# Attention scores as two 128-row products a head, last keys' weights stacked over 128 rows, and four pairs of heads instead of eight with values in whole float32

## The chip, the cores and the metric

The kernel runs on one core of one Trainium2 chip. The metric is the device time of one execution in microseconds. Its engines are TensorE (PE: matrix products; its weight loads are listed apart as PEld), VectorE (DVE), ScalarE (ACT), GpSimd (POOL) and the sync engine (SP), which issues nearly all DMAs here.

## The reference

Causal attention with a decay, then two feed-forward layers:

```python
scores = q @ k.T / 8 + cum[i] - cum[j]   # cum = cumsum(log(clip(f, 1e-4, 1))), keys j > i masked
attn = softmax(scores);  x = attn @ v    # 4 batches, 8 heads, 576 tokens, head dimension 64
x = (sigmoid(x @ w_gate) * (x @ w_val)) @ w_out      # 2304 tokens, 512 -> 1536 -> 512
h = x @ w_in;  out = (h * clip(h + 3, 0, 6) / 6) @ w_out2   # 512 -> 2048 -> 512
```

The weights arrive as float64 bits; everything else is float32.

## The kernel before, in words

**Numbers.** A float32 value is carried as two float32r parts, hi and lo, whose sum is exact, and a product is hi·hi + hi·lo + lo·hi: three TensorE products. `mm3` (L496) does this in the layers.

**Attention.** The work is 16 pairs of heads (`Pair`, pair 0 to 15), four to a batch. A pair has five steps: query tiles 0 to 3 of 128 queries with 128, 256, 384 and 512 keys, and the last 64 queries of both heads side by side ("the last queries") with all 576 keys. The steps run as a pipeline over `units` (L777 to L820): while step t makes scores (`scores`, L319) and exponentials (`expo`, L355: VectorE adds the decay and takes the row minimum, ScalarE exponentiates), step t-1 is normed (`norm`, L386, a GpSimd product), step t-2 is transposed on TensorE (`flip`, L393, with copies out of PSUM by ScalarE), and step t-3's weights meet the values (`values`, L439). Two thirds into a pair, `prep` (L233) transposes the next pair's q and k and splits them.

**Three settings by pair number (L742).** Pairs 0 to 7 (`WH`) take weights times values in float32 as it is, which the trace lists as two TensorE instructions a product; later pairs split the weights (VectorE, L436) and the values (GpSimd, `split_v`) into hi and lo. Pairs 0 to 6 (`UP`) run the steps from the first to the last, and a mask product on TensorE (L341) hides later keys; later pairs run them backwards, and GpSimd overwrites the decay instead (`hide`, L302). Pairs 0 to 6 (below `TW`) make a head's scores from three products over 64 rows (L337), the two heads in the upper and lower 64 rows. Pairs 7 to 15 stack q's hi and lo rows to 128 rows, stack k's hi twice (`stack_k`, on VectorE and GpSimd), and take one product over 128 rows (L326) and one over 64 rows with k's lo (L331). The last queries' scores are three products over 128 rows for each half of the keys, with q's hi and lo in block-diagonal tiles `qbd` (L348).

**What fills TensorE.** A weight's conversion takes three VectorE, two ScalarE or GpSimd steps and one more subtraction (`convert`, L95; while attention runs, GpSimd makes hi and lo, L61 and L62); 18 of them are spread over the steps from step 5 on. When they are done and a batch's attention is stored, groups of the gated layer's first part (`Filler`; tiles `pg`, `pv`, `po`; products of 256 columns) are put between attention's products; what is left of them follows after attention. Then come the rest of the gated layer (`ff1b`) and the second layer (`ff2`).

**Order.** The scheduler of the framework sets each engine's order when the program is built, from a simulated timeline; on the chip every engine runs its list in that order.

Of the kernel before, what the change touches and what calls it, by code (L numbers as in the profile page):

```python
# [12 lines left out]
ALU = mybir.AluOpType  # L13
# [7 lines left out]
def attn_moe_kernel(  # L21
# [33 lines left out]
    # float32 values are carried as two float32r parts, hi + lo, whose sum is exact;  # L55
    # a product is hi*hi + hi*lo + lo*hi.
# [21 lines left out]
    # rows 0..63 repeated in rows 64..127, for the two heads' last queries  # L78
# [14 lines left out]
    # A weight comes as float64 bits: float32 has the same sign, the exponent less 896 (a  # L93
    # product with 2^-112 of the high word read as float32), and the leading 23 mantissa bits.
# [18 lines left out]
    class Converter:  # L113
        """Weight halves still to be loaded and converted; run() emits some of them."""
# [4 lines left out]
        def cols(self, pool, tag, w, c0, nm):  # L119
            """256 columns of w, for products over its rows."""  # L120
# [6 lines left out]
        def rows(self, pool, tag, w, r0, nm):  # L127
            """256 rows of w."""
# [28 lines left out]
    ep = att.enter_context(tc.tile_pool(name="ep", bufs=7))  # L157
# [4 lines left out]
    qbd = [[const.tile([P, P], F32R, name=f"qbd{i}{j}") for j in range(2)] for i in range(2)]  # L162
    for i in range(2):
        for j in range(2):
            nc.vector.memset(qbd[i][j].bitcast(F32), 0.0)

    def cumulate():
        """Cumulative log decay, to DRAM."""
# [10 lines left out]
    def load_nat(src, b, hp, c0, c1, nm):  # L179
        """Rows c0 * 128 to c1 * 128, or to the end."""  # L180
        t = nat.tile([P, NKT, 2, D], F32, tag="nat", name=nm)
        n = min(c1, NQ)
        for j in range(2):
            nc.sync.dma_start(
                t[:, c0:n, j, :],
                src[b, 2 * hp + j, c0 * P : n * P, :].rearrange("(c p) d -> p c d", p=P),
            )
        if c1 > NQ:
            nc.sync.dma_start(
                t[:TAIL, NQ, :, :],  # L190
                src[b, 2 * hp : 2 * hp + 2, NQ * P : S, :].rearrange("h p d -> p h d"),
            )
        return t

    class Pair:
        """Two heads of one batch; its steps are the query tiles 0..3 and the last 64 queries, or
        some of them."""

        def __init__(self, i, b, hp, order, whole, two):
            self.i, self.b, self.hp, self.order, self.whole, self.two = i, b, hp, order, whole, two  # L200
            self.s0, self.s1 = min(order), max(order) + 1
            self.tail = self.s1 > NQ
            self.c0, self.c1 = self.s0 * P, S if self.tail else self.s1 * P
            # values' parts, after the steps that they wait for
            self.parts = {}
            for part, ss in ((0, (0, 1)), (1, (2, 3, NQ))):
                if ss[0] in order:
                    self.parts[max(ss, key=order.index)] = part
            self.x = None
            self.up = order[0] < order[-1]  # L210
            self.pemask = self.up or i < PM

        def load(self):
            self.qn = load_nat(q, self.b, self.hp, self.s0, self.s1, "qn")
            self.kn = load_nat(k, self.b, self.hp, 0, self.s1, "kn")
            self.vn = load_nat(v, self.b, self.hp, 0, self.s1, "vn")

        def load_decay(self):
            h0 = self.b * H + 2 * self.hp
            self.dc = a2.tile([P, 2, NQ * P], F32, tag="dc", name="dc")  # L220
            n = min(self.c1, NQ * P)
            for j in range(2):
                nc.sync.dma_start(self.dc[:, j, :n], cum_d[h0 + j : h0 + j + 1, :n].to_broadcast([P, n]))
# [9 lines left out]
        def prep(self):  # L233
            # q and k with head dimension on partitions, both heads; scores are negated
            q0, n = self.c0, min(self.c1, NQ * P)
            tq = psB.tile([P, 512], F32, tag="B", name="tq")
# [658 lines left out]
```

## Time and profile before

| | us |
|---|---|
| device time, median of 3 runs | 1126.88 (1120.99 to 1127.61) |
| the profiled execution: span from first to last instruction | 1124.5 |
| TensorE busy in the span | 1110.0 (99%) |
| VectorE, ScalarE, GpSimd busy | 592.4, 399.3, 339.7 |
| largest lines of the chain that ended last | TensorE 88%, VectorE 4%, DMA 3% |

The profiled execution's own time is its span of 1124.5 us, and no more of it is shown; it lies 2.4 us under the median and inside the range of the runs. Busy time on TensorE counts an instruction from its start to a modelled end, so neighbours overlap; what a product costs is read from one start to the next. Attention runs to about 395 us, the filling groups to about 500 us, the two layers to the end.

### The profile page before, as it was taken

What the parts mean: (1) busy time and instruction counts of PE and PEld (TensorE: products, weight loads), DVE (VectorE), ACT (ScalarE), POOL (GpSimd) and SP (SyncE); (2) the same over time, 40 slices, a digit from 0 to 9 for tenths busy, and PEclk for the clock granted to TensorE, in tenths of its full rate; (3) what the DMA queues carried; (4) which work ended last, traced back from release to release, by engine and by line L of the source; (5) the groups of instructions that cost most, each with busy time, mean ns of one, the idle gap of its engine ahead of it and who ended that gap; (6) DMA issues with size and microseconds to landing.
All of it is one profiled execution on the core that took longest, in us unless ns stands there. A gap on an engine that the chain in (4) does not pass through costs nothing.

```text
span 1124.5 us, 17493 instructions
## 1 busy us (share of the span) xinstructions
PE 1110.0 (99%) x6351; PEld 932.0 (83%) x6351; DVE 592.4 (53%) x1329; ACT 399.3 (36%) x937; POOL 339.7 (30%) x500
## 2 busy tenths in 40 slices
PE   8999999999999999999999999999999999999998
PEld 4666778988889999998888888987888888888897
DVE  4788865767666457421253453698333333333343
ACT  4767655565555345330121222343121111121121
POOL 2687775666575534110030321222000000000000
PEclk8999999999999999999999999999999999999999
DMA  7578653263531276420346252752200210110010
GB/s 200 146 213 253 188 160 113 84 170 90 154 104 65 80 256 207 138 94 1 131 131 219 98 189 88 241 163 89 75 38 1 74 39 1 45 50 1 15 43 19
DMA packets 121909, 125.54 MB, mean 112 GB/s; under 512 B 63648, under 2 KB 81056, under 8 KB 121824
## 3 DMA queue, kind: packets, MB, share of 16 engines
q1 hardware_dynamic: 121728, 124.29, 35.7%
q8 instruction: 50, 0.82, 0.3%
q14 instruction: 35, 0.29, 0.1%
q10 hardware_dynamic: 96, 0.15, 0.0%
HBM read 96.02 MB, written 28.39 MB: 111 GB/s over the span
## 4 chain that ended last, share of the span: by engine, by line
PE 88%; DVE 4%; DMA 3%; issue 2%; POOL 1%; ACT 1%; ACTq 0%; SPq 0%; POOLq 0%; DVEq 0%
PE po L497 9%; PE po L499 9%; PE po L498 9%; PE pv L471 7%; PE ph L498 5%; PE ph L499 5%; PE ph L497 5%; PE pv L497 4%; PE pg L498 4%; PE pg L497 4%; PE pv L499 4%; PE pg L499 4%; PE pv L498 4%; PE st L337 3%; PE tt L418 2%; PE st L331 2%
## 5 line engine op out<-in xcount | busy, mean ns | idle before, releaser
L59 ACT CAST ga<-sg 128x512 fp32r<-128x512 f32 (+1 forms) x80 | 46.2, 577 | 291.3 <-DVE sg L713 285.2
L712 DVE TENSOR_SCALAR sg<-ph 128x512 f32<-128x512 f32 (+1 forms) x80 | 51.0, 637 | 155.8 <-PE ph L499 155.8
L497 PE MATMUL po<-w,ga 128*128 128x512 f32 x288 | 112.5, 391 | 1.2 <-ACT ga L59 1.1
L498 PE MATMUL po<-w,ga 128*128 128x512 f32 x288 | 112.3, 390 | 0.0
L62 DVE TENSOR_TENSOR ga<-sg,ga 128x512 fp32r<-128x512 f32 (+1 forms) x110 | 72.1, 656 | 70.8 <-ACT ga L59 49.4
L391 POOL TENSOR_SCALAR e<-e,m 128x256 f32<-128x256 f32 (+4 forms) x144 | 86.5, 613 | 64.8 <-DVE m L389 24.0
L499 PE MATMUL po<-w,ga 128*128 128x512 f32 x288 | 102.2, 391 | 0.9 <-DVE ga L62 0.8
L366 ACT ACTIVATE e<-e,m 128x256 f32<-128x256 f32 (+4 forms) x144 | 84.1, 585 | 41.8 <-DVE m L360 32.5
L360 DVE CUSTOM_DVE_ANT_0 e<-st,dc 128x128 f32<-128x128 f32 (+3 forms) x128 | 61.0, 486 | 42.1 <-PE st L331 16.7
L498 PE MATMUL ph<-xb,wi 128*128 128x512 f32 (+1 forms) x224 | 80.3, 359 | 0.0
L499 PE MATMUL ph<-xb,wi 128*128 128x512 f32 (+1 forms) x224 | 80.3, 359 | 0.0
L497 PE MATMUL ph<-xb,wi 128*128 128x512 f32 (+1 forms) x224 | 80.0, 359 | 0.0
L61 POOL TENSOR_SCALAR ga<-sg 128x512 fp32r<-128x512 f32 (+1 forms) x30 | 20.9, 697 | 159.5 <-DVE sg L677 159.5
L105 ACT ACTIVATE raw<-raw 128x512 f32<-128x512 f32 x68 | 46.5, 684 | 62.8 <-DVE raw L102 57.1
L497 PEld LDWEIGHTS po<-w,ga 128*128 128x128 f32 x288 | 54.1, 188 | 12.8 <-ACT ga L59 2.3
L677 DVE TENSOR_TENSOR sg<-sg,pv 128x512 f32<-128x512 f32 (+1 forms) x30 | 18.9, 631 | 86.9 <-PE pv L499 86.9
L499 PEld LDWEIGHTS po<-w,ga 128*128 128x128 f32 x288 | 53.4, 188 | 13.3 <-DVE ga L62 2.4
L497 PE MATMUL pv<-x,wv 128*128 128x256 f32 x216 | 63.0, 291 | 0.8 <-DVE sg L569 0.8
L498 PEld LDWEIGHTS po<-w,ga 128*128 128x128 f32 x288 | 54.2, 188 | 10.6
L497 PE MATMUL pg<-x,wg 128*128 128x256 f32 x216 | 62.4, 290 | 0.0
L498 PE MATMUL pg<-x,wg 128*128 128x256 f32 x216 | 62.0, 287 | 0.0
L499 PE MATMUL pv<-x,wv 128*128 128x256 f32 x216 | 62.0, 287 | 0.0
(188 smaller groups left out, 3044.1 us busy)
## 6 DMA issues: line engine op xcount, KB each, us to landing
raw<-in_moe_w_out_dram SPq DMA_DIRECT2D x28, 512.0 KB, 3.8
xb<-x_d SPq DMA_DIRECT2D x44, 256.0 KB, 4.3
x<-x_d SPq DMA_DIRECT2D x18, 512.0 KB, 4.6
dc<-cum_d SPq DMA_DIRECT2D x32, 256.0 KB, 4.0
raw<-in_moe_w_in_dram SPq DMA_DIRECT2D x16, 512.0 KB, 4.7
x_d<-xs SPq DMA_DIRECT2D x32, 256.0 KB, 2.2
raw<-in_moe_w_gate_dram SPq DMA_DIRECT2D x12, 512.0 KB, 5.0
raw<-in_moe_w_val_dram SPq DMA_DIRECT2D x12, 512.0 KB, 4.2
```

What stands on the lines that cost most here:

```text
L59: nc.scalar.copy(hi, src)
L62: eng_lo.tensor_tensor(lo, src, hi.bitcast(F32), ALU.subtract)
L105: nc.scalar.activation(e, e, AF.Copy, scale=2.0**-112)
L337: nc.tensor.matmul(self.sts[j][:, :n], l[r, s * P : n], r_[r, :n], start=(a == 0), stop=(a == 2 and not self.pemask))
L360: pace["dve"] = nc.vector.tensor_tensor_reduce(out=e, in0=st, in1=d, op0=ALU.add, op1=ALU.min, scale=1.0, scalar=3.0e38, accum_out=m[:, a ...
L366: nc.scalar.activation(e, e, AF.Exp, bias=m[:, a : a + 1], scale=-1.0, accum_out=m[:, 2 + a : 3 + a])
L391: nc.gpsimd.tensor_scalar(e, e, m[:, 6 + j : 7 + j], 1.0, ALU.mult, ALU.mult)
L471: nc.tensor.matmul(o[r, q0:], w[:p0, kt], e, start=(kt == 0 and a == 0), stop=(kt == nk - 1 and a == na - 1),)
L497: nc.tensor.matmul(o, wh, xh, start=first, stop=False)
L498: nc.tensor.matmul(o, wh, xl, start=False, stop=False)
L499: nc.tensor.matmul(o, wl, xh, start=False, stop=last)
L712: nc.vector.tensor_scalar(sg, ph, 3.0, 0.0, ALU.add, ALU.max)
```

## The change

Every pair now makes scores in two products over 128 rows: q's hi and lo rows stacked (`qs`), against k's hi in both halves (`kh`), then against k's lo in both halves (`kl`). `prep` writes k's hi and lo of each head into that head's half, and GpSimd copies each to the other half (four instructions of 64 rows by 576 columns a pair); `stack_k` is gone. The last queries' scores are four products a half, two a head, with hi and lo rows stacked in `qz`. In split pairs, the last 64 keys' weights lie over 128 rows, hi below and lo above, with the values loaded twice, so that one product of 128 rows takes the place of two of 64 rows. `WH` and `UP` are 4: pairs 4 to 15 split weights and values, and run backwards with GpSimd's hiding in place of the mask product. The pool of exponentials has 6 buffers, not 7.

```diff
-    ep = att.enter_context(tc.tile_pool(name="ep", bufs=7))
+    ep = att.enter_context(tc.tile_pool(name="ep", bufs=6))
...
-            self.pemask = self.up or i < PM
+            self.pemask = self.up
...
+            self.qn = nat.tile([P, NKT, 2, D], F32, tag="nat", name="qn")
...
+            self.kn = load_nat(k, self.b, self.hp, "kn", ((0, k), (TAIL, q)))
+            self.vn = load_nat(v, self.b, self.hp, "vn", ((0, v), (TAIL, v)))
...
         def prep(self):
...
+            for (r, ro), t in zip(rs, self.qs):
+                nc.scalar.activation(t[r], tq[r], AF.Copy, scale=sc)
+                nc.vector.scalar_tensor_tensor(t[ro], tq[r], sc, t[r].bitcast(F32), ALU.mult, ALU.subtract)
...
+            for (r, ro), kh, kl in zip(rs, self.kh, self.kl):
+                for cs, t in ((slice(0, NQ * P), tk[r]), (slice(NQ * P, S), tl[r, :TAIL])):
+                    nc.scalar.copy(kh[r, cs], t)
+                    nc.vector.tensor_tensor(kl[r, cs], t, kh[r, cs].bitcast(F32), ALU.subtract)
+                for t in (kh, kl):
+                    nc.gpsimd.tensor_scalar(t[ro], t[r].bitcast(F32), 1.0, 1.0, ALU.mult, ALU.mult)
...
-        def stack_k(self):
...
         def scores(self, s):
...
-                for a, (l, r_) in enumerate(((self.qh, kh), (self.qh, kl), (self.ql, kh)) if not self.two else ()):
-                    for j in range(2):
-                        r = slice(64 * j, 64 * j + 64)
-                        nc.tensor.matmul(
-                            self.sts[j][:, :n], l[r, s * P : n], r_[r, :n], start=(a == 0), stop=(a == 2 and not self.pemask)
-                        )
...
+                for j, st in enumerate(self.sts):
+                    nc.tensor.matmul(st[:, :n], self.qs[j][:, qs], self.kh[j][:, :n], start=True, stop=False)
+                    nc.tensor.matmul(
+                        st[:, :n], self.qs[j][:, qs], self.kl[j][:, :n], start=False, stop=not self.pemask
+                    )
...
-                nc.tensor.transpose(t5[:TAIL, :P], e[:, NQ * P :], ident)
+                nc.tensor.transpose(t5[:, :P], e[:, S - P :], ident)
...
+                last = self.etB[0][:, :, NQ - 1, 0:TAIL]
+                jobs.append(([last[TAIL:], last[:TAIL]], t5[TAIL:, :P].rearrange("p (j b) -> p j b", j=2)))
...
+                        ks = slice(TAIL, P) if self.whole else slice(0, P)
+                        jobs.append((w[ks, kt], q0, ets[0][ks, j, NQ - 1, 0:TAIL]))
...
-    WH, UP, TW, PM = 8, 7, 7, 0
+    WH, UP = 4, 4
```

TensorE's list in a late pair, around the scores of 384 keys. Before (L326 and L331 are the 128-row and the 64-row scores, L471 the values, L411 transposes):

```order
L326 MATMUL st<-ks,qh 128x384
L326 MATMUL st<-ks,ql 128x384
L331 MATMUL st<-kl,qh 128x384
L471 MATMUL pv<-etB,vs 128x320 x6
L471 MATMUL pv<-etB,vs 128x192 x2
L471 MATMUL pv<-etB,vs 128x64 x2
L411 MATMUL tt<-ident,e 128x128 x2
L331 MATMUL st<-kl,ql 128x384
L326 MATMUL st<-ks,qh 128x256
L331 MATMUL st<-kl,qh 128x256
```

The same place in the changed program (L299 and L300 are the scores with `kh` and `kl`, L432 the values, L455 to L457 a filling group):

```order
L299 MATMUL st<-kh,qs 128x512
L300 MATMUL st<-kl,qs 128x512
L455 MATMUL pv<-x,wv_718 128x256
L299 MATMUL st<-kh,qs 128x384
L300 MATMUL st<-kl,qs 128x384
L456 MATMUL pv<-x,wv_718 128x256
L457 MATMUL pv<-x,wv_718 128x256
L432 MATMUL pv<-etB,vs 128x320 x6
L432 MATMUL pv<-etB,vs 128x192 x2
L432 MATMUL pv<-etB,vs 128x64
L299 MATMUL st<-kh,qs 128x384
L300 MATMUL st<-kl,qs 128x384
```

A head's two scores now stand together and none of the products is over 64 rows; the values' last row is one product, not two.

GpSimd's list in pair 5, before (L391 the norm, L61 and L62 hi and lo of a converted weight `wv`, `wo` or of the stored `x`):

```order
L391 TENSOR_SCALAR e<-e,m 128x128 x2
L61 TENSOR_SCALAR wv_1318<-raw 128x512
L391 TENSOR_SCALAR e<-e,m 128x256 x2
L62 TENSOR_TENSOR wv_1318<-raw,wv_1318 128x512
L391 TENSOR_SCALAR e<-e,m 128x384 x2
L391 TENSOR_SCALAR e<-e,m 128x512 x2
L61 TENSOR_SCALAR xh<-x 128x576
L61 TENSOR_SCALAR wo_1452<-raw 128x512
L62 TENSOR_TENSOR x<-x,xh 128x576
L62 TENSOR_TENSOR wo_1452<-raw,wo_1452 128x512
L61 TENSOR_SCALAR wo_1452<-raw 128x512
```

The changed program at the end of pair 4 and the first step of pair 5 (L354 the norm, L261 the copies of k, L290 and L285 the hiding, L61 and L62 on `vs` the split values):

```order
L261 TENSOR_SCALAR kh<-kh 64x576
L61 TENSOR_SCALAR wv_1394<-raw 128x512
L261 TENSOR_SCALAR kl<-kl 64x576
L261 TENSOR_SCALAR kh<-kh 64x576
L62 TENSOR_TENSOR wv_1394<-raw,wv_1394 128x512
L261 TENSOR_SCALAR kl<-kl 64x576
L354 TENSOR_SCALAR e<-e,m 128x128 x2
L290 AFFINE_SELECT dc<-dc 128x2x128
L285 AFFINE_SELECT dt<-dt 64x64 x2
L290 AFFINE_SELECT dc<-dc 128x2x128
L61 TENSOR_SCALAR vs<-vn 128x5x64 x2
L354 TENSOR_SCALAR e<-e,m 128x576
```

Beside norms and conversions there now stand copies of k, hiding and splitting. In TensorE's list, the products of the filling groups that come ahead of pair 8's first q transpose are 252 before and 180 in the changed program.

## Rows read from the trace of the kernel before

**Rows 1.** Page: span, and busy time of each engine (share of the span) x instructions.

```profile
span 1124.5 us, 17493 instructions
...
PE 1110.0 (99%) x6351; PEld 932.0 (83%) x6351; DVE 592.4 (53%) x1329; ACT 399.3 (36%) x937; POOL 339.7 (30%) x500
```

**Rows 2.** Windows: start:end us, length, busy us (instructions) PE, PEld, DVE, ACT, POOL, clock, DMA.

```profile
70.00:88.00 18.00, 17.70 (x105) 11.38 (x104) 13.90 (x46) 12.74 (x38) 13.66 (x17) 1.00 0.69 193
...
193.00:347.00 154.00, 154.00 (x1096) 136.75 (x1095) 102.55 (x325) 88.23 (x242) 99.75 (x197) 1.00 0.42 119
395.00:501.00 106.00, 105.16 (x872) 104.51 (x871) 59.67 (x105) 48.28 (x105) 31.09 (x23) 1.00 0.55 175
500.00:700.00 200.00, 200.00 (x901) 166.28 (x900) 74.11 (x113) 40.49 (x65) 34.95 (x37) 1.00 0.36 120
```

**Rows 3.** Windows of line 497 alone: the filling groups’ first products in six pairs.

```profile
193.00:347.00 154.00, 58.28 (x196) 36.99 (x196) 1.00 0.42 119
```

**Rows 4.** Timeline, TensorE, pair 11: start us, us to a modelled end, instruction.

```profile
258.30 0.44 PE L326 MATMUL st<-ks,qh 128*128 128x384 f32 x1
258.58 0.34 PE L326 MATMUL st<-ks,ql 128*128 128x384 f32 x1
258.85 0.44 PE L331 MATMUL st<-kl,qh 64*128 64x384 f32 x1
259.22 1.68 PE L471 MATMUL pv<-etB,vs 128*128 128x320 f32 x10
```

**Rows 5.** Timeline, TensorE, pair 3 to 4: three-product scores, and values in whole float32.

```profile
69.80 0.50 PE L337 MATMUL st<-kh,qh 64*128 64x512 f32 x1
...
70.85 0.50 PE L337 MATMUL st<-kh,qh 64*128 64x512 f32 x1
...
72.53 2.15 PE L471 MATMUL pv<-etB,vn 128*64 128x320 f32 x8
...
75.20 2.66 PE L471 MATMUL pv<-etB,vn 64*64 64x64 f32 x12
```

**Rows 6.** Page, costliest groups: GpSimd’s norm (count, busy us, mean ns).

```profile
L391 POOL TENSOR_SCALAR e<-e,m 128x256 f32<-128x256 f32 (+4 forms) x144 | 86.5, 613 | 64.8 <-DVE m L389 24.0
```

**Rows 7.** Groups by line and form, GpSimd: the other work of a pair.

```profile
L62 POOL TENSOR_TENSOR x<-x,xh 128x576 fp32r<-128x576 f32 x16 | 22.8, 1425 | 0.5
...
L62 POOL TENSOR_TENSOR wg<-raw,wg 128x512 fp32r<-128x512 f32 x12 | 17.0, 1423 | 10.4 <-ACT wg L59 10.2
...
L315 POOL TENSOR_SCALAR_AFFINE_SELECT dc<-dc 128x256 f32<-128x256 f32 x36 | 15.3, 425 | 34.5 <-DMA dc<-cum_d 20.2 <-DVE m L360 10.2 <-DVE m L389 1.8
...
L290 POOL TENSOR_SCALAR ks<-kh 64x512 fp32r<-64x512 f32 x18 | 12.0, 667 | 1.5
L62 POOL TENSOR_TENSOR vs<-vn,vs 128x256 fp32r<-128x256 f32 x16 | 11.5, 734 | 0.0
L61 POOL TENSOR_SCALAR xh<-x 128x576 fp32r<-128x576 f32 x16 | 10.7, 672 | 12.1 <-issue 7.4 <-ACT x L477 4.7
L61 POOL TENSOR_SCALAR vs<-vn 128x256 fp32r<-128x256 f32 x16 | 6.9, 446 | 4.1 <-PE pv L471 3.3 <-DMA vn<-in_v_dram 0.8
...
L310 POOL TENSOR_SCALAR_AFFINE_SELECT dt<-dt 64x64 f32<-64x64 f32 x18 | 4.7, 259 | 12.1 <-DMA dt<-cum_d 6.9 <-DVE raw L102 4.6 <-PE st L331 0.2
...
L61 POOL TENSOR_SCALAR wg<-raw 128x512 fp32r<-128x512 f32 x6 | 4.0, 659 | 3.4 <-DVE m L388 2.6 <-DVE raw L108 0.7
```

**Rows 8.** Timeline, GpSimd: the last norms of pair 0 and of pair 7.

```profile
29.75 0.75 POOL L391 TENSOR_SCALAR e<-e,m 128x576 f32<-128x576 f32 x1 [0.86 <-DVE m L389]
...
176.43 0.73 POOL L391 TENSOR_SCALAR e<-e,m 128x128 f32<-128x128 f32 x2 [1.81 <-DVE m L389]
```

**Rows 9.** Timeline, VectorE: one form of instruction twice, 2 us apart.

```profile
72.90 1.11 DVE L388 TENSOR_SCALAR m<-m 128x2 f32<-128x2 f32 x1
...
74.82 0.15 DVE L388 TENSOR_SCALAR m<-m 128x2 f32<-128x2 f32 x1
```

**Rows 10.** Windows at the start: the same columns.

```profile
10.00:14.00 4.00, 2.85 (x15) 1.44 (x15) 0.94 (x7) 1.63 (x4) 0.00 (x0) 1.00 1.00 247
14.00:18.00 4.00, 4.00 (x13) 2.06 (x12) 1.97 (x10) 2.58 (x10) 1.66 (x4) 0.61 0.77 176
```

More of the change, by code (lines that the diff above doesn't have):

```diff
@@ L278, in stack_k @@
-        def stack_k(self):
-            if not self.two:
-                return
-            self.ks = [a1.tile([P, NQ * P], F32R, tag=f"ks{j}", name="ks") for j in range(2)]
-            for j, t in enumerate(self.ks):
-                for g in range(2):
-                    o, i = t[64 * g : 64 * g + 64], self.kh[64 * j : 64 * j + 64, : NQ * P]
-                    eng = EK[2 * j + g]
-                    if eng is nc.scalar:
-                        eng.copy(o, i.bitcast(F32))
-                    else:
-                        eng.tensor_scalar(o, i.bitcast(F32), 1.0, 1.0, ALU.mult, ALU.mult)
+            for c in range(NQ):
+                nc.tensor.transpose(tq[:, c * P : (c + 1) * P], self.qn[:, c].rearrange("p h d -> p (h d)"), ident)
@@ new lines, in prep @@
+            tk = psB.tile([P, 512], F32, tag="B", name="tk")
+            tl = psB.tile([P, 512], F32, tag="B", name="tl")
+            for c in range(NKT):
+                t = tk[:, c * P : (c + 1) * P] if c < NQ else tl[:, :P]
+                nc.tensor.transpose(t, self.kn[:, c].rearrange("p h d -> p (h d)"), ident)
+            for (r, ro), kh, kl in zip(rs, self.kh, self.kl):
[4 more added lines that the diff above has]
+                    nc.gpsimd.tensor_scalar(t[ro], t[r].bitcast(F32), 1.0, 1.0, ALU.mult, ALU.mult)
@@ L395, in flip @@
             es = self.es[s]
[L396 to L403 removed]
+            dt, parts = (F32, 1) if self.whole else (F32R, 2)
+            if s == next(x for x in self.order if x < 2):
+                self.etA = [et.tile([P, 2, 384], dt, tag=f"etA{x}", name="etA") for x in range(parts)]
+            if s == next(x for x in self.order if x >= 2):
+                self.etB = [et.tile([P, 2, NQ, 320], dt, tag=f"etB{x}", name="etB") for x in range(parts)]
             jobs = []
@@ L763, in attn_moe_kernel @@
     pairs = [
-        Pair(i, i // NP, i % NP, list(range(NQ + 1) if i < UP else range(NQ, -1, -1)), i < WH, i >= TW)
+        Pair(i, i // NP, i % NP, list(range(NQ + 1) if i < UP else range(NQ, -1, -1)), i < WH)
         for i in range(B * NP)
@@ L771, in attn_moe_kernel @@
     pairs[0].load_decay()
[L772 to L773 removed]
+    pairs[0].load_tail_decay()
     warm_up(WU)
@@ L789, in attn_moe_kernel @@
             p.expo(s)
-            if i == 0:
-                p.stack_k()
             if s > 0:
                 p.hide(s - 1)
-            if nxt and nxt.tail and i == (len(p.order) - 1 if p.up else 2):
+            if nxt and i == (len(p.order) - 1 if p.up else 2):
                 nxt.load_tail_decay()
```

179 lines of the change are left out of this document (59 added, 120 removed).

## The prediction

> **What bounds the kernel now.** I read the page first: TensorE is busy for 1110.0 of 1124.5 us, and the next engine for 592.4 [rows 1]. That is too coarse, since the change touches attention alone, so I cut attention into stretches. Around pair 4 (70 to 88 us) TensorE is busy for 17.7 of 18 us, with VectorE at 13.9 and GpSimd at 13.7 of the 18: TensorE bounds, with little room beside it. In pairs 9 to 14 (193 to 347 us) it is busy throughout, and GpSimd for 99.75 of 154: TensorE bounds, with much room [rows 2]. A busy TensorE is not one at its best rate. Filling groups alone, 395 to 501 us, run 872 products of 256 columns in 106 us, 0.122 us each, and 512 columns take 200 / 901 = 0.22 us [rows 2]. Six late pairs hold 3 x 196 filling products [rows 3], 71.5 us at that rate; the other 82.5 us are attention's, 13.75 us a pair.
>
> **What a product over 64 rows costs.** The starts in rows 4 show it. Of three scores of 384 keys, the first, right behind a 64-row product, takes 0.28 us, the second, ahead of one, 0.27, and the third, over 64 rows, 0.37. By columns (between 0.122 and 0.22) each should take 0.17. So a 64-row product standing alone costs 0.10 ahead of it, 0.20 itself and 0.11 behind: 0.41 us over a 128-row product in its place [rows 4].
>
> **Late pairs, 8 to 15.** The change removes the eight 64-row scores and the two groups of 64-row values of a pair: ten places, 4.1 us. It adds two products of 288 columns for the last queries, 0.14 each by columns, and drops two of 64 columns and one small transpose, about as much. Some 64-row products already stood together and shared a change of shape, and I take 0.3 off: 3.8 us a pair. The bounds are 3.0 (a third of the places shared) and 4.2. Eight pairs: **-30 us**. Pair 7 falls partly behind the point that I use below; its scores, and its values in whole float32 (2.15 + 2.66 = 4.8 us less a modelled overlap [rows 5], against some 2.3 split: 2368 columns a head at 0.122 for 256), give **-2**.
>
> Here stands a rule against the change. In this trace the two heads' 64-row scores stand apart, so each takes its full time. The Trainium skill (TensorE: Matmul & The Clock Gate, Part 3) says that products on different row groups run side by side in the array, almost for the price of one. By it the old scores would already be nearly free of their second head and the late pairs' gain would vanish; the starts in rows 4, with 0.37 us for one such product before anything else begins, do not show it here.
>
> **What hides the late gain.** It pays only while TensorE stays the bound. GpSimd, at 16.6 us a late pair, gets four copies of k and loses two. A copy of 64x512 takes 0.667 us [rows 7], so 0.75 for 576 columns: +3.0 - 1.3 = 1.7 us, 18.3 in all. A pair then needs 13.75 - 3.8 + 107 filling products x 0.122 = 23 us, so GpSimd is at 80%. It norms the weights that TensorE transposes next in a fixed list; I charge waits of **+3** (bounds 0 and 8).
>
> **The first half, pairs 1 to 7.** TensorE's work falls here too. A head's scores of 512 keys with mask take 70.85 - 69.80 = 1.05 us [rows 5] and then need some 0.5; over a pair that is about 3.5 us, and pairs 4 to 6 lose 2.4 of float32 values and the masks besides. I cost all this at nothing, because GpSimd becomes the bound. Its sum for the seven pairs, in means: nine norms of 0.613 are 5.5 [rows 6] and a store 0.67 + 1.43 = 2.1, 53 together for seven pairs; 18 conversions of 0.66 + 1.42 are 37.5; the copies of k 7 x 3.0 = 21; in pairs 4 to 7 the hiding, 4 x 0.425 + 2 x 0.259 = 2.2, and the splitting, 2 x (0.446 + 0.734) x 320/256 = 2.95, together 21; and six filling groups' splits ahead of that point, 128x256 like the values', 7 [rows 7]. Total 139.5 us. The check on this method: norms, store and three conversions come to 13.8 for a pair, and pair 4's stretch shows 13.66 [rows 2].
>
> From pair 0's last norm to pair 7's the kernel takes 177.2 - 30.5 = 146.7 us today [rows 8]. GpSimd's 139.5 fit in only if it never waits; from 97% busy down to 84% they take 144 to 166 us. I take 90%, nearest to an engine that bounds but waits for norms and conversions: 155, **+8** (bounds -3 and +20). VectorE also gets more there (k's lo in two halves, the weights' lo from pair 4 on) and stays a little below GpSimd.
>
> Behind that point 72 more filling products are left, 252 - 180 by TensorE's lists, since the changed order puts fewer ahead of it: 72 x 0.122 = **+9**. The smaller pool of exponentials and k's copies in the prologue I put at nothing: the first scores wait for the decay anyhow; if not, they cost a few us, which the bounds hold. Both layers are untouched.
>
> **The sum.** -30 - 2 + 3 + 8 + 9 = -12 to -13 us on the profiled span of 1124.5, which is 1112. The span lies 2.4 us below the median of the runs, so I put the same difference on 1126.9: **1114 us**.
>
> **The rivals.**
>
> *A: the first half costs nothing* (0.22). GpSimd packs well, or short steps of TensorE shorten the chain of each step. For it: GpSimd's sum is still 7 us below today's time. Against it: it must be 95% busy or more. -30 - 2 + 2 + 9 - 4 = -25: 1102 us.
>
> *B: the first half loses what the second gains* (0.22). VectorE and GpSimd get in each other's way: the same small VectorE instruction takes 1.11 us at 72.90 and 0.15 at 74.82 [rows 9], and both engines would be nearly full in pairs 4 to 7. A tenth on GpSimd's sum is 14 us: -30 - 2 + 3 + 22 + 9 = +2: 1129 us. This decides if pairs 1 to 7 take over 165 us. The Trainium skill (GPSIMD Engine Reference, Key points) says that GpSimd shares its SBUF interfaces with VectorE and contends with its fast modes and two-input instructions; the two rows agree, without telling how often.
>
> *C, slower: TensorE's clock falls in pairs 4 to 7* (0.09). In 10 to 14 us TensorE was busy for 2.85 of 4 us, and then the granted clock was 0.61 of 2.4 GHz, on its way to 1.2 [rows 10]. In pairs 4, 5 and 7 TensorE would have some 10 to 13 us of work in 21 or more, as idle as it was there. At 1.2 GHz its 10 us become 20, in a chain with GpSimd's: 4 us more for each of four pairs, and 150 filling products that the list puts around pair 6 take up to 18 more, of which I count 8. +8 becomes +32: 1138 us. It decides if the granted clock is under 0.8 over the four pairs. Against it: pair 1's and 2's TensorE has no such gaps, and filling products stand in the way in pair 6.
>
> *D: side by side* (0.02). If the 64-row scores did overlap as in the rule above, only the values would save, about 0.8 us a pair: -6 + 3 + 8 + 9 = +14: 1141 us.
>
> **How the numbers follow.** The forecast has 0.45, and its own bounds reach from 1100 to 1130 at worst, mostly 1106 to 1122. A tells from no change at about 1% (11.3 us: under 1115.6 is faster, over 1138.1 slower), which is what a measurement of this kernel can tell. Of the forecast's 0.45 some 0.28 lie under 1115.6 and 0.17 above. Faster: 0.28 + 0.22 = 0.50. Slower: half of C and most of D, and a little of B: 0.09. The rest, 0.41, is within 1%. The range from 1098 to 1134 holds the forecast, A and B nearly whole and leaves out C and D and the ends of A: some 0.15 to 0.2.
>
> **What would show it.** Right: in the late pairs no 64-row score, scores of 384 keys at about 0.17 us from start to start, and attention's share 10 us a pair; in pairs 4 to 7 GpSimd busy for nine tenths and TensorE with gaps that end on norms or copies of k; pair 7's last norm at about 185 us. Wrong: late pairs with TensorE gaps of over 1 us a pair, a pair 7 that ends before 177 or after 197 us, or a granted clock well below 1 between 90 and 180 us.

## The result, and the profile after

The changed kernel takes 1140.02 us (1139.22 to 1143.81), the kernel before on the same chip 1127.24: a ratio of 1.0138, 95% interval 1.0099 to 1.0177. It is slower by 13 us, where 12 us less were forecast. The page of the changed kernel, against [rows 1]:

```profile
span 1137.6 us, 17589 instructions
...
PE 1074.4 (94%) x6260; PEld 939.8 (83%) x6260; DVE 622.2 (55%) x1398; ACT 419.3 (37%) x984; POOL 382.7 (34%) x548
```

TensorE has 36 us less to do and the span is 13 us longer: it waits. I cut both traces at three points (pair 8's first q transpose, attention's last product with the values, the last filling product), and count a filling product at the 0.122 us of [rows 2]:

| us | before | after | difference |
|---|---|---|---|
| start to pair 8's first q transpose (177 and 180 filling products ahead of it) | 168.6 | 198.2 | +29.6 |
| to attention's last product | 222.4 | 200.6 | -21.8 |
| the same, less 867 and 882 filling products | 116.6 | 93.0 | -23.6 |
| to the last filling product | 109.7 | 115.9 | +6.2 |
| the same, less 900 and 882 products | -0.1 | 8.3 | +8.4 |
| to the end | 623.9 | 623.0 | -0.9 |

One execution of the run called hybrid below, the profiled one, was disturbed (1168 us, its clock at 0.86), and its row gives the median of the five others.

**The late pairs** gained. The same place as in [rows 4], TensorE's timeline in a late pair of the changed kernel, two heads' scores of 384 keys:

```profile
285.90 0.34 PE L299 MATMUL st<-kh,qs 128*128 128x384 f32 x1
286.07 0.34 PE L300 MATMUL st<-kl,qs 128*128 128x384 f32 x1
286.25 0.34 PE L299 MATMUL st<-kh,qs 128*128 128x384 f32 x1
286.42 0.33 PE L300 MATMUL st<-kl,qs 128*128 128x384 f32 x1
286.60 0.28 PE L457 MATMUL pv<-x,wv 128*128 128x256 f32 x1
```

From start to start they take 0.17 to 0.18 us, the time by columns, with nothing added.

**The first half** lost. Windows from pair 0's last norm to pair 7's, first of the kernel before, then of the changed one (busy us and instructions of PE, PEld, DVE, ACT, POOL; granted clock; DMA):

```profile
30.30:176.90 146.60, 144.51 (x915) 102.85 (x915) 112.94 (x324) 95.43 (x262) 110.33 (x147) 1.00 0.65 192
```

```profile
27.30:209.70 182.40, 140.44 (x859) 116.11 (x859) 134.24 (x381) 110.11 (x289) 141.72 (x197) 0.85 0.55 159
...
93.40:209.70 116.30, 88.50 (x574) 79.37 (x574) 89.62 (x242) 67.21 (x175) 90.35 (x131) 0.85 0.52 150
```

The stretch grew from 147 to 182 us. TensorE was the bound (99%) and is now busy for 77%, though part of that at half rate; GpSimd is at 78%, VectorE at 74%. No engine is full. What TensorE waited for in this stretch, before (three of its four lines) and after (the five longest; what waited and what ended it: us in total, times, longest):

```profile
PE pv L497 <- DVE sg L569: 0.8, 1, 0.8
PE tt L418 <- DVE kl L268: 0.5, 2, 0.3
PE st L337 <- ACT kh L267: 0.4, 1, 0.4
```

```profile
PE tt L374 <- DVE qs L250: 11.0, 3, 3.8
PE st L299 <- DVE m L323: 7.9, 8, 2.3
PE tt L388 <- POOL e L354: 7.8, 3, 4.9
PE tt L381 <- POOL dc L290: 4.0, 1, 4.0
PE tt L381 <- DVE qs L250: 3.1, 1, 3.1
```

2 us of waits became 42. The longest group is a transpose of weights (L374) behind VectorE's split of q (L250). It reads nothing of q: it wants a PSUM bank, and q's and k's transposes (`tq`, `tk`, `tl`) hold all three of that pool until the split has read `tq`. On TensorE during pair 3:

```profile
81.04 0.33 PE L255 MATMUL tl<-ident,kn 128*128 128x128 f32 x1 [0.46 <-ACT etA L396]
84.95 1.08 PE L374 MATMUL tt<-ident,e 128*128 128x128 f32 x4 [3.58 <-DVE qs L250]
```

From the first transpose of k to the last reading of it the bank was held for 2.0 to 3.3 us in pairs 1 to 5 before, and for 5.0 to 7.4 us now. The split is longer because each head now has its own instructions, and those over 64 rows are no shorter: VectorE takes 0.69 us for k's lo at 64x512 now and took 0.69 at 128x512 before, ScalarE 0.58 for k's hi at either. After such a wait the clock falls, as the windows around it show:

```profile
80.00:84.00 4.00, 0.92 (x6) 0.55 (x5) 3.94 (x8) 3.62 (x11) 4.00 (x7) 0.82 0.66 140
84.00:88.00 4.00, 2.35 (x10) 1.86 (x10) 3.81 (x12) 1.73 (x5) 3.81 (x5) 0.50 0.76 217
88.00:92.00 4.00, 4.00 (x18) 2.83 (x17) 1.03 (x4) 1.74 (x5) 3.74 (x6) 0.50 0.91 341
```

In the last of these TensorE is busy throughout, at 1.2 GHz. Ahead of pair 8 the clock is low in five such stretches of 44 us together, and in a sixth of 10 us that ends at its start.

**Behind attention** TensorE waits too, 1.8 us at the longest, and the clock falls once more (windows of the changed kernel; in [rows 2] the same place ran at 1.00):

```profile
396.00:400.00 4.00, 2.10 (x15) 1.52 (x13) 1.54 (x4) 1.52 (x4) 0.00 (x0) 1.00 0.02 4
400.00:406.00 6.00, 5.13 (x24) 5.17 (x25) 0.70 (x2) 0.38 (x1) 2.08 (x2) 0.50 0.91 272
```

### The profile page after: what moved, and what is told of

Read it like the earlier page. It is cut to its first block, busy times and chain, and to the rows that moved or that the text cites. A ratio compares the mean times of both kernels' runs of the same rounds, so it can differ in the third digit from the quotient of the medians.

```text
span 1137.6 us, 17589 instructions
## 1 busy us (share of the span) xinstructions
PE 1074.4 (94%) x6260; PEld 939.8 (83%) x6260; DVE 622.2 (55%) x1398; ACT 419.3 (37%) x984; POOL 382.7 (34%) x548
## 4 chain that ended last, share of the span: by engine, by line
PE 75%; DVE 8%; DMA 6%; POOL 5%; issue 5%; ACT 2%; SPq 0%; ACTq 0%; POOLq 0%; DVEq 0%
PE po L455 9%; PE po L456 9%; PE po L457 9%; PE ph L457 5%; PE ph L456 5%; PE ph L455 5%; PE pv L432 4%; PE pg L455 4%; PE pv L455 4%; PE pg L457 4%; PE pg L456 4%; PE pv L457 4%; PE pv L456 4%; DMA dt<-cum_d 2%; DVE e L323 2%
## 5 line engine op out<-in xcount | busy, mean ns | idle before, releaser
L455 PE MATMUL po<-w,ga 128*128 128x512 f32 x288 | 112.5, 391 | 1.2 <-ACT ga L59 1.1
L62 DVE TENSOR_TENSOR ga<-sg,ga 128x512 fp32r<-128x512 f32 (+1 forms) x110 | 72.1, 656 | 70.6 <-ACT ga L59 49.2
L457 PE MATMUL po<-w,ga 128*128 128x512 f32 x288 | 102.2, 391 | 0.5 <-DVE ga L62 0.4
L329 ACT ACTIVATE e<-e,m 128x256 f32<-128x256 f32 (+3 forms) x144 | 84.0, 584 | 38.6 <-DVE m L323 34.8
L354 POOL TENSOR_SCALAR e<-e,m 128x256 f32<-128x256 f32 (+4 forms) x144 | 84.1, 594 | 33.3 <-DVE m L352 8.2
L323 DVE CUSTOM_DVE_ANT_0 e<-st,dc 128x128 f32<-128x128 f32 (+3 forms) x128 | 61.1, 487 | 47.5 <-POOL dc L290 14.9
L457 PE MATMUL ph<-xb,wi 128*128 128x512 f32 (+1 forms) x224 | 80.3, 359 | 0.0
L455 PE MATMUL ph<-xb,wi 128*128 128x512 f32 (+1 forms) x224 | 80.0, 359 | 0.0
L61 POOL TENSOR_SCALAR ga<-sg 128x512 fp32r<-128x512 f32 (+1 forms) x30 | 21.1, 703 | 158.5 <-DVE sg L635 158.5
L455 PE MATMUL po<-gall,wo 128*128 128x256 f32 x216 | 62.4, 298 | 4.7 <-DVE x L442 1.8
L455 PEld LDWEIGHTS po<-w,ga 128*128 128x128 f32 x288 | 54.1, 188 | 12.9 <-ACT ga L59 2.3
L456 PE MATMUL po<-gall,wo 128*128 128x256 f32 x216 | 62.3, 294 | 2.0 <-DVE gall L62 2.0
L457 PEld LDWEIGHTS po<-w,ga 128*128 128x128 f32 x288 | 53.5, 188 | 12.9 <-DVE ga L62 1.9
L455 PE MATMUL pv<-x,wv 128*128 128x256 f32 x216 | 62.6, 290 | 1.3 <-DVE sg L527 1.3
L455 PE MATMUL pg<-x,wg 128*128 128x256 f32 x216 | 63.3, 293 | 0.2 <-DVE x L442 0.2
```

Of the source, the lines that this page charges most:

```text
L61: eng_hi.tensor_scalar(hi, src, 1.0, 1.0, ALU.mult, ALU.mult)
L62: eng_lo.tensor_tensor(lo, src, hi.bitcast(F32), ALU.subtract)
L323: pace["dve"] = nc.vector.tensor_tensor_reduce(out=e, in0=st, in1=d, op0=ALU.add, op1=ALU.min, scale=1.0, scalar=3.0e38, accum_out=m[:, a ...
L329: nc.scalar.activation(e, e, AF.Exp, bias=m[:, a : a + 1], scale=-1.0, accum_out=m[:, 2 + a : 3 + a])
L354: nc.gpsimd.tensor_scalar(e, e, m[:, 6 + j : 7 + j], 1.0, ALU.mult, ALU.mult)
L455: nc.tensor.matmul(o, wh, xh, start=first, stop=False)
```

## The experiments

All ratios are against the kernel before, run on the same chip beside them. "First half" is the stretch from pair 0's last norm to pair 7's, with GpSimd's busy share and TensorE's granted clock in it.

| kernel | us | ratio (95% interval) | first half, us | GpSimd | clock |
|---|---|---|---|---|---|
| before | 1127.2 | | 146.6 | 75% | 1.00 |
| changed | 1140.0 | 1.014 (1.010 to 1.018) | 182.4 | 78% | 0.85 |
| scores_only | 1128.9 | 1.001 (1.000 to 1.003) | 169.2 | 75% | 0.90 |
| settings_only | 1150.8 | 1.020 (1.016 to 1.024) | 167.6 | 76% | 0.90 |
| wh4_up7 | 1139.6 | 1.013 (1.010 to 1.016) | 181.1 | 76% | 0.87 |
| wh8_up4 | 1139.6 | 1.011 (1.008 to 1.014) | 178.8 | 75% | 0.88 |
| k_copies_scalar | 1144.1 | 1.015 (1.012 to 1.019) | 181.4 | 68% | 0.86 |
| tensor_kept_busy | 1138.1 | 1.010 (1.007 to 1.013) | 182.4 | 78% | 0.89 |
| bank_after | 1144.3 | 1.016 (1.011 to 1.020) | 181.5 | 79% | 0.86 |
| bank_scores | 1131.5 | 1.004 (1.002 to 1.006) | 163.6 | 78% | 0.93 |
| split_scores | 1121.8 | 0.995 (0.993 to 0.997) | 160.5 | 80% | 0.93 |
| copy_scores | 1153.2 | 1.023 (1.018 to 1.028) | 179.2 | 74% | 0.84 |
| scores_warm | 1125.8 | 1.001 (0.999 to 1.002) | 163.3 | 77% | 0.99 |
| before_ep6 | 1138.5 | 1.009 (1.007 to 1.012) | 152.1 | 73% | 0.99 |
| e_after | 1144.5 | 1.015 (1.012 to 1.018) | 170.4 | 79% | 0.86 |
| e_scores | 1139.5 | 1.012 (1.008 to 1.015) | 162.0 | 75% | 0.88 |
| hybrid | 1103.1 | 0.981 (0.978 to 0.985) | | | |
| hybrid_again | 1109.2 | 0.985 (0.982 to 0.987) | 152.5 | 73% | 0.99 |
| hybrid_e | 1119.7 | 0.993 (0.991 to 0.996) | 148.2 | 73% | 0.94 |
| hybrid_prep | 1122.3 | 0.994 (0.991 to 0.997) | 163.9 | 77% | 0.92 |

### The two halves of the change apart

scores_only, the changed kernel with the old settings:

```diff
-    WH, UP = 4, 4
+    WH, UP = 8, 7
```

> The changed kernel with the settings of before (pairs 0 to 7 with values in whole float32, pairs 0 to 6 forwards with the mask product); scores, copies of k and stacked last keys stay. Theory 1 (hiding and splitting from pair 4 on overload GpSimd and VectorE): their 21 us of GpSimd work are gone, pair 8's first q transpose comes at 165 to 172 us and not 198, the whole at 1105 to 1113 us. Theory 2 (the copies of k and short TensorE steps are the fault, in all of pairs 1 to 7): pair 8 starts at 185 us or later, the whole at 1125 us or more.

settings_only, the kernel before with the new settings:

```diff
-    WH, UP, TW, PM = 8, 7, 7, 0
+    WH, UP, TW, PM = 4, 4, 7, 0
```

> The kernel before with only its settings changed: pairs 4 to 15 split weights and values, run backwards and hide on GpSimd, while pairs 0 to 6 keep three products a score and nothing copies k there. Theory 1 (the settings overload GpSimd and VectorE by themselves): pair 8's first q transpose moves from 169 to 185 us or later, the whole comes to 1140 us or more. Theory 2 (the copies of k are needed for the loss): GpSimd has 15 us less than in the changed kernel, pair 8 starts at 172 us or earlier, the whole is 1123 to 1130 us.

Pair 8 starts at 185.4 us in scores_only, which is theory 2's sign there, and at 184.8 in settings_only, 0.2 short of theory 1's. Each half alone makes it 16 to 17 us late, so neither is the only cause. scores_only gets 23.2 us back in the late pairs and loses 9.6 behind attention, so the new scores alone come to nothing. settings_only loses another 8.5 us, less filling products, in the late pairs, whose settings did not change; why is open. The settings cost 23 us on the old scores and, from scores_only to the changed kernel, 11 on the new ones.

### Which setting

```diff
-    WH, UP = 4, 4
+    WH, UP = 4, 7     # wh4_up7
+    WH, UP = 8, 4     # wh8_up4
```

> The changed kernel with pairs 4 to 6 forwards with the mask product as before (UP = 7), but weights and values split from pair 4 on (WH = 4). Theory 1 (turning the order round at pair 4, with the wait for the last queries' decay and the hiding, is the settings' cost): 1128 to 1132 us, like scores_only at 1128.9. Theory 2 (splitting weights and values in pairs 4 to 7 is the cost): 1137 to 1142 us, like the changed kernel.

> The counterpart: the changed kernel with values in whole float32 in pairs 0 to 7 (WH = 8), and pairs 4 to 15 backwards with hiding (UP = 4). Theory 1 (the order and the hiding): 1137 to 1142 us. Theory 2 (the splitting): 1127 to 1132 us. If both carry a share, both of these kernels lie between 1131 and 1137 us.

Both lie at 1139.6, like the changed kernel. Either setting alone brings the 11 us, and the second adds nothing that these runs can tell, which neither theory had. The traces show that the two do add in part: less filling products, pair 8 starts 8 and 10 us later than in scores_only, and 13 with both, but with both the late pairs gain 23.6 us, not 14.5 and 17.1.

### GpSimd's load

```diff
-                    nc.gpsimd.tensor_scalar(t[ro], t[r].bitcast(F32), 1.0, 1.0, ALU.mult, ALU.mult)
+                    nc.scalar.copy(t[ro], t[r].bitcast(F32))
```

> The changed kernel with the four copies of k a pair on ScalarE in place of GpSimd: GpSimd loses about 3 us a pair, ScalarE gets about as much. If GpSimd's load sets the time of pairs 1 to 7 (21 us of it go): pair 8's first q transpose at 178 to 185 us, the whole at 1120 to 1127 us. If the lowered clock sets it, with GpSimd only following: 195 us or later, and 1135 us or more. If ScalarE takes GpSimd's place as the bound: slower than 1140 us.

```profile
26.80:208.20 181.40, 144.28 (x876) 117.24 (x875) 134.31 (x382) 127.61 (x323) 123.59 (x169) 0.86 0.56 162
```

GpSimd has 123.6 us to do in place of 141.7, ScalarE 127.6 in place of 110.1, and the stretch is 1 us shorter. Moving GpSimd's load does not shorten it, though the forecast of the first half rested on that load. It can't be said from this run alone that the load is free: ScalarE took it over, and 1144 us is what the third expectation (ScalarE as the new bound) gives as well.

### The clock

tensor_kept_busy adds to the changed kernel, and scores_warm to scores_only (there with `range(4)` and steps 5 to 41):

```diff
+            if 8 <= t < 40:
+                for _ in range(2):
+                    o = psF.tile([P, 512], F32, tag="F", name="warm")
+                    for c in range(0, 512, P):
+                        nc.tensor.matmul(o[:, c : c + P], identb, mask, start=True, stop=True)
```

> The changed kernel with eight needless products of 128x128 in each of the steps 8 to 39 (256 in all, at 0.11 us each 28 us of TensorE work that nothing reads), spread by the scheduler over its waiting time. If the lowered clock is what costs (TensorE's products take twice their time in 55 us of the 198): the granted clock stays above 0.95 between 60 and 198 us, pair 8's first q transpose comes at 180 to 188 us, the whole at 1122 to 1130 us. If GpSimd and VectorE set the time and TensorE has slack at either clock: the clock rises as well, but pair 8 starts at 195 to 203 us and the whole stays at 1137 to 1146 us.

> The kernel with the settings of before and the new scores (scores_only, 1128.9 us, pair 8 at 185 us), with sixteen needless products of 128x128 in each of the steps 5 to 41, to fill TensorE's waits. If the lowered clock costs what its share of the chain says (TensorE's pieces of the chain of waits lie 18 us in stretches at 1.2 GHz, half of that would be saved): granted clock above 0.97 between 35 and 185 us, pair 8 at 175 to 180 us, the whole at 1119 to 1124 us. If the waits for banks and for the other engines are all there is: pair 8 at 183 us or later, 1127 us or more.

The first raised the clock of the stretch only from 0.85 to 0.89 and tells little. The second brought it to 0.99. It is 3 us faster than scores_only by the medians, but hardly by the ratios to the kernel before (1.0005 and 1.0013), and its stretch is 6 us shorter:

```profile
27.60:190.90 163.30, 154.82 (x1375) 122.93 (x1375) 110.97 (x339) 106.06 (x279) 125.27 (x163) 0.99 0.58 170
```

TensorE is 95% busy here, with 43 us of needless products in the whole (592, 0.073 us each from start to start), and the order puts 84 filling products ahead of pair 8, not 180. Less filling products, pair 8 starts 7 us later than in scores_only. So this bounds nothing from above: what the clock gave, the needless work may have taken. A full clock beside such filler gained little here.

### The PSUM banks

bank_after, and bank_scores on scores_only:

```diff
+            pool, tag = (psF, "F") if self.i <= 5 else (psB, "B")
-            tq = psB.tile([P, 512], F32, tag="B", name="tq")
+            tq = pool.tile([P, 512], F32, tag=tag, name="tq")      # and tk likewise
-    FV = lambda p: p.i < 5
+    FV = lambda p: False
```

> The changed kernel with the transposed q and k of pairs 0 to 5 in the two PSUM banks of the filling groups, and all values in the three banks that the transposes of the weights use. Theory 1 (q's and k's transposes now hold two of those three banks for 6 to 7 us a pair, since the split takes two ScalarE and two VectorE instructions each where one each was enough, and the weights' transposes wait for a bank): TensorE's waits of 3 to 4 us for line L250 go away in pairs 1 to 4, pair 6 starts its q transposes at 118 to 125 us and not 131.8, the whole at 1125 to 1133 us. Theory 2 (VectorE and GpSimd have too much to do, and the bank is only where it shows): the waits move to scores and norms, pair 6 at 129 us or later, the whole at 1136 to 1144 us.

> The same exchange of banks in the kernel with the settings of before (scores_only, pair 6 at 123.1 us, 1128.9 us). Theory 1 (banks): pair 6 at 108 to 114 us, the whole at 1112 to 1120 us. Theory 2 (VectorE's and GpSimd's work): pair 6 at 120 us or later, the whole at 1126 us or more.

split_scores, on scores_only: `prep` is cut in two, k's part stays in its place, and q's goes a step ahead:

```diff
                 if nxt:
-                    nxt.prep()
+                    nxt.prep_k()
+            if nxt and p.order.index(s) == 1:
+                nxt.prep()
```

> The kernel with the settings of before (scores_only), with q's transposes and split one step earlier than k's, in all pairs, so that they do not hold two banks at once; no instruction is added or left out. Theory 1 (banks): one bank more is free, pair 8 starts its q transposes' successor at 170 to 178 us in place of 185, the whole at 1113 to 1121 us. Theory 2 (VectorE's and GpSimd's work): nothing is saved, 1126 us or more.

copy_scores, on scores_only:

```diff
+            qf, kf = (x.rearrange("p c h d -> p (c h d)")[:, : NQ * P] for x in (self.qn, self.kn))
+            nc.scalar.activation(qf, tq, AF.Copy, scale=sc)
...
+            nc.scalar.copy(kf, tk)      # the splits read qf and kf
```

> The kernel with the settings of before (scores_only), where one ScalarE copy of 128 rows each brings the transposed q and k out of their banks, over the used q and k, and the splits read that; 1.2 us more of ScalarE a pair. Theory 1 (banks): the banks are held 1 to 2.5 us in place of 4 to 7, TensorE's waits for L250 go away, the whole at 1110 to 1120 us. Theory 2 (the engines' work): ScalarE and the chain from k to the scores get longer, 1130 to 1140 us.

In bank_after the waits for L250 are nearly gone, and others have come. TensorE's waits there (L300 and L324 are L299 and L323 of the changed kernel, L251 its L250):

```profile
PE st L300 <- DVE m L324: 15.4, 11, 3.7
PE po L458 <- POOL wo L62: 3.1, 2, 1.8
...
PE tt L382 <- DVE qs L251: 1.7, 1, 1.7
```

The stretch stays at 181.5 us, and pair 6 starts at 145 us in bank_after and at 127 in bank_scores: theory 2's signs in both. No bank was added, since the values now stand in the three; the longest wait is now for VectorE to read the scores out of theirs. So the bank was where the wait showed, and other banks did not remove it. copy_scores held the banks for 1.2 to 2.6 us and was the slowest of all, slower than either theory had. Only spreading q's and k's preparation over two steps paid, 7 us, and that moved VectorE's and ScalarE's work as well as the banks. Of the 10 us between its trace and that of scores_only, 9 lie behind attention and, less filling products, 2.6 in attention, so it says little about the first half.

### The pool of exponentials

```diff
-    ep = att.enter_context(tc.tile_pool(name="ep", bufs=7))
+    ep = att.enter_context(tc.tile_pool(name="ep", bufs=6))     # before_ep6: the kernel before with this alone
```

> The kernel before with one thing changed: 6 buffers of exponentials in place of 7. Theory 1 (a step needs up to six at once, so a seventh is what lets the next step begin, and its lack couples VectorE to TensorE's transposes): VectorE waits for transposes of older weights, pair 8 starts at 175 us or later in place of 169, the whole at 1133 to 1145 us. Theory 2 (six are enough; only the new split of q and k is the cost): 1124 to 1130 us, no change.

e_after, e_scores and hybrid_e take buffers by the size of the step:

```diff
-                es = [ep.tile([P, S], F32, tag="e", name="e")[:, :n] for j in range(2)]
+                tag, w, nb = ((f"e{s}", n, 2), ("e2", NQ * P, 4))[s >= 2]
+                es = [ep.tile([P, w], F32, tag=tag, bufs=nb, name="e")[:, :n] for j in range(2)]
```

> The changed kernel with the exponentials in buffers of their own size: two each for the steps of 128 and 256 keys, four for those of 384 and 512, one for the last queries; 9 buffers in less room than the 6. Theory 1 (buffers of exponentials): VectorE's waits of 17 us for line L374 and its like shrink to under 5, pair 8's q transposes start at 180 to 188 us in place of 198, the whole at 1120 to 1130 us. Theory 2 (the split's work and the settings): 1135 to 1145 us. The two last-query steps in a row at pairs 3 and 4 now share one buffer and cost up to 3 us under either.

> The same buffers in the kernel with the settings of before (scores_only, 1128.9 us, pair 8 at 185 us). Theory 1: pair 8 at 168 to 175 us, the whole at 1108 to 1118 us. Theory 2: 1125 to 1132 us.

> The same buffers in the hybrid (three-product scores in pairs 0 to 6, two-product scores in pairs 7 to 15, settings of before; 1105.4 us). Theory 1: the hybrid's first half also ran with six buffers, so it gains 3 to 8 us: 1097 to 1102 us. Theory 2: 1103 to 1108 us.

One buffer less, which I had put at nothing, costs the kernel before 10 us (1.0094), as theory 1 had it: pair 8 starts 5.5 us later, the late pairs take 2.4 more, the stretch behind attention 3.8. The scheduler's order changed with it (1062 filling products ahead of attention's end, not 1044). Some of VectorE's waits from 30 to 185 us, the scores' minimum (it writes the buffer) for transposes of older weights:

```profile
DVE e L360 <- PE tt L411: 3.6, 4, 2.1
...
DVE e L360 <- PE t L427: 3.3, 2, 2.6
...
DVE e L360 <- PE tt L418: 2.1, 2, 1.2
```

9.0 us, against 0.9 in the kernel before. The buffers by size shortened the first half of the changed kernel by 12 us and made the rest longer; with one buffer for the last queries they are another pool, not a larger one, and don't tell what six buffers cost in the changed kernel. All three kernels are slower than those that they start from (e_after by 4 us, e_scores by 11, hybrid_e by 11 to 17), the last two by more than either theory had.

### The hybrid

Old split and three products for pairs 0 to 6, new scores for 7 to 15, settings of before:

```diff
-    WH, UP = 4, 4
+    WH, UP, TW = 8, 7, 7
+            if self.i < TW:
+                (qh, ql), kh, kl = self.qs, self.kh[0], self.kl[0]
+                nc.scalar.activation(qh, tq, AF.Copy, scale=sc)
+                nc.vector.scalar_tensor_tensor(ql, tq, sc, qh.bitcast(F32), ALU.mult, ALU.subtract)
...
+                    for a, (l, r_) in enumerate(((qh, kh), (qh, kl), (ql, kh))):
```

> Pairs 0 to 6 as in the kernel before (three products over 64 rows a score, one ScalarE and one VectorE instruction each to split q and k, nothing copied), settings of before; pairs 7 to 15 with the two-product scores, the copies of k and the stacked last keys. Theory 1 (the two-product scores pay where TensorE is the bound and cost where the steps wait for one another): pair 8 starts at 166 to 172 us as before, the late pairs give 20 to 24 us, behind attention 4 to 9 are lost again, the whole at 1106 to 1115 us. Theory 2 (the loss of the first half comes from the smaller pool of exponentials or from the order, not from the form of the scores): pair 8 at 180 us or later, the whole at 1122 us or more.

> The hybrid once more, unchanged: 1101 to 1108 us, pair 8's q transposes at 166 to 172 us, TensorE busy for 95% or more of pairs 1 to 7, and no wait of TensorE over 1 us there.

hybrid_prep adds the long split to pairs 0 to 6, with GpSimd's four copies of k, which no product reads there:

```diff
-                nc.scalar.activation(qh, tq, AF.Copy, scale=sc)
-                nc.vector.scalar_tensor_tensor(ql, tq, sc, qh.bitcast(F32), ALU.mult, ALU.subtract)
+                for r, _ in rs:
+                    nc.scalar.activation(qh[r], tq[r], AF.Copy, scale=sc)
+                    nc.vector.scalar_tensor_tensor(ql[r], tq[r], sc, qh[r].bitcast(F32), ALU.mult, ALU.subtract)
...
+                    for t, u in ((kh, self.kh[1]), (kl, self.kl[1])):
+                        nc.gpsimd.tensor_scalar(u[ro], t[r].bitcast(F32), 1.0, 1.0, ALU.mult, ALU.mult)
```

> The hybrid with the long split in pairs 0 to 6 as well: q's and k's hi and lo in two ScalarE and two VectorE instructions of 64 rows in place of one each, and four GpSimd copies of k a pair that no product reads; scores stay at three products. Theory 1 (the long split is the cost of the two-product form): 1120 to 1130 us. Theory 2 (TensorE's shorter work is: its gaps, and the clock that falls in them): 1104 to 1111 us. In between if each carries a share.

The hybrid beats both kernels, by 1.5 to 1.9% against before in its two runs: the late pairs' 22 us are kept (94.4 us less filling products against 116.6), pair 8 starts at 171.7, and behind attention 0.8 us are lost (these by the trace of hybrid_again, whose 1109.2 us lie 1.2 above what was expected). TensorE is busy for 146.8 of 152.5 us of its first half and for 114.8 of 116.2 us of pairs 10 to 14:

```profile
29.80:182.30 152.50, 146.81 (x934) 107.25 (x934) 106.32 (x328) 99.09 (x268) 111.61 (x147) 0.99 0.68 199
...
217.90:334.10 116.20, 114.82 (x927) 112.93 (x926) 83.86 (x262) 75.34 (x210) 84.15 (x151) 1.00 0.49 140
```

Going on to scores_only costs 20 to 26 us by the medians, against the two runs of the hybrid; hybrid_prep has 13 to 19 of these, and 7 lie between it and scores_only. The traces tell where. Pair 8 starts at 185.5 us in hybrid_prep and at 185.4 in scores_only, 14 us behind the hybrid: the long split, copies included, is all of the first half's loss, and the shorter products add nothing to it there. The 7 us lie behind attention, where hybrid_prep loses 1.5 us and scores_only 9.4. Which part of the long split counts, the instructions over 64 rows or the copies, no run tested.

In hybrid_prep the cost stands in the trace as a lower clock. TensorE waits for 5.9 us of the first half, and for 5.5 in hybrid_again; but it works for 27.2 us at half rate there, against 3.4. Half of what is more, 12 us, is my estimate of what a full clock would have saved, and the two profiled executions are 12.7 us apart. The ten runs order themselves by the mean clock over the whole execution, which alone would not tell cause from effect:

```
clock 0.981 to 0.983: 1121.97 to 1123.77 us (six runs)
clock 0.986 to 0.988: 1117.37, 1118.13, 1118.46 us
clock 0.995:          1111.45 us
```

The last is at the hybrid's clock (0.991 to 0.998) and 0.7 us above the slowest of its second run (1107.21 to 1110.72). The profiled execution has a stretch of 14 us with TensorE busy throughout at half rate:

```profile
64.00:68.00 4.00, 3.88 (x22) 2.54 (x21) 3.91 (x14) 3.51 (x11) 3.67 (x6) 0.67 0.81 232
68.00:82.00 14.00, 13.96 (x43) 8.46 (x43) 6.38 (x25) 6.82 (x18) 5.85 (x8) 0.50 0.29 100
```

## Why the prediction was wrong

**The step that failed** is the first half: "I cost all this at nothing, because GpSimd becomes the bound", and "I take 90%": +8 us, where this stretch took 36 us more, and 29.6 more had passed when pair 8 began. GpSimd's sum was right, 139.5 us forecast and 141.7 measured. Its share was not: GpSimd was busy for 75% of this stretch before and lies between 73 and 80% in every trace of the table but that of the kernel that took work off it. I read 13.66 of 18 us [rows 2] for a check of the sum and not as the share that this pipeline reaches; at 76% the forecast would have been 184 us, and 182.4 came. That would have been the right number for a wrong reason: with 18 us of GpSimd's work moved to ScalarE nothing is gained, and no engine is full. What the runs put in its place: the long split of q and k, of which the forecast priced only GpSimd's copies (13 to 19 us in the hybrid), and either of the settings (11 us on the new scores) make TensorE wait for VectorE, GpSimd and banks in turn, and behind such waits its clock was at half. The forecast had no term for waits that pass from engine to engine, and left the clock to a rival.

**Late pairs.** The mechanism was right, the size was not: -23.6 us, where -30 was forecast. Of these, 2.0 are pair 7's values (5.5 us before, 3.5 a pair after), which the forecast has in its -2; that leaves 2.7 a pair, against 3.8 with a lower bound of 3.0. The term that was too large is the 0.41 us for a 64-row score. From start to start over pairs 8 to 15, the scores of 128 to 512 keys take 36.0 us before and 21.7 after for 128 products each, 64 of them changed: 0.22 us each, without what a 64-row product costs a product behind it that is no score. The values' two places came as priced: those of queries 256 to 575 gave 6.5 us over the eight pairs, against 6.6.

Part of the reason is that the two heads' 64-row products do not always stand apart. Where one follows the other, they run side by side, as here in the kernel before:

```profile
183.48 0.34 PE L326 MATMUL st<-ks,ql 128*128 128x384 f32 x1
183.75 0.44 PE L331 MATMUL st<-kl,qh 64*128 64x384 f32 x1
183.75 0.44 PE L331 MATMUL st<-kl,ql 64*128 64x384 f32 x1
184.12 0.39 PE L499 MATMUL pg<-x,wg 128*128 128x256 f32 x1
```

The two start within 4 ns of each other, and the next product starts 0.37 us later, as it does behind a single one in [rows 4]. So the rule behind rival D, which the prediction did not find in [rows 4], does hold in this trace. From pair 8 on, 6 of the 32 couples of heads stand so; the others stand apart and take their full time, which is why removing them paid. What is left of the difference between 0.41 and 0.22 is open, and so is what an order would give that puts all couples side by side: no run tested it.

**Waits late, +3:** none to speak of; TensorE is busy for 141.9 of 143.3 us in pairs 9 to 14.

**Deferred filling, +9:** a mistake in reading the list. 252 products stand ahead of pair 9's first q transpose in the kernel before; ahead of pair 8's there are 177, against 180. The statement in the section on the change has the same slip. The term is nothing. In its place 8.4 us came behind attention, from waits and the clock. The kernels with 1062 filling products ahead of attention's last product lose 1.5 to 10.9 us there; those with 1044 lose nothing (-0.1 to 0.8). That a longer lead leaves nothing to fill with while the last pair is stored is my reading, which no run tested alone.

**The pool of exponentials, at nothing:** 10 us in the kernel before. Its part in the changed kernel is open.

**The rivals.** D's 1141 us came nearest to the 1140.0, by luck: it has 6 us for the late pairs, which gained 23.6. C gave 1138 us and the side, and the clock did fall, but not as deep as C asked (0.85 over pairs 4 to 7, not under 0.8) and not there alone; its sum also holds -30 for the late pairs and +9 for filling that was not deferred, so its nearness is in part luck. B's condition, pairs 1 to 7 in over 165 us, was met with 182; GpSimd's own sum did not grow, so its reason fell. A is out.

**What stays open** is how much of the 30 us is the clock. In the changed kernel 54.5 us up to 210 are at half rate, and TensorE is busy for 39.1 of them. At full rate these would take half, so the clock is at most some 20 us of the 30, by this estimate, and waits are at least 10. The two runs with needless products raised the clock and took TensorE's time at once, and don't tell more.

## What to carry to other kernels

Make a change that saves TensorE's time and gives work to the other engines only where those have room and TensorE stays the bound. TensorE was the bound in both halves before. The same scores gained 22 us in the late pairs, where GpSimd was busy for two thirds, and their long split lost 14 in the first seven, where it was at 75% already; taking them in the late pairs alone gave the fastest kernel. In a pipeline of short steps with few buffers, count on no more of an engine that is not the bound than the busy share that it has shown there, 73 to 80% for GpSimd here, and don't count on idle time of four engines at once. Count instructions in two lists from the same landmark, and price a buffer that is taken away.

## What the runs showed of the hardware

Two TensorE products over 64 rows each, one on the upper and one on the lower half, started within 4 ns of each other and together took the 0.37 us of one (384 columns, in the kernel before, at 183.75 us).

An instruction over 64 rows took as long as one over 128, in means: VectorE 0.69 us (k's lo, 512 columns) and ScalarE 0.58 us (k's hi), in the changed kernel over 64 rows and in the kernel before over 128; GpSimd 0.68 to 0.71 us over 64 rows and 0.68 over 128 at 576 columns, both in the changed kernel.

The clock fell behind short waits, and stayed low longer than they had lasted. Behind attention, waits of 0.6, 0.3 and 1.8 us were followed by 6.8 us at a granted clock of 0.5. In hybrid_prep a stretch of 17 us was at 0.5 with TensorE busy nearly throughout, behind two waits of 0.32 and 0.35 us, and one of 10 us behind a wait of 2.2 us. Over its runs a fall of the mean clock from 0.995 to 0.981 went with 12 us, 1.1% of the time for 1.4% of the clock.
